# Block mask by matmul for the first two chunks, a second order of the batch 0 loads, and one PSUM tensor with planned banks

## The chip, the cores and the metric

The kernel runs on one core of a Trainium2 chip. The metric is the device time of one execution in microseconds (us), and the number given for a kernel is the median over its runs. The profile comes from one execution of its own. Its span is counted from the first to the last instruction, so it is a little shorter than the time of the same execution.

Engines are named as in the profile: PE multiplies matrices (PEld are its weight loads), DVE is the vector engine, ACT the scalar engine with the activation functions, POOL is GpSimd, SP issues transfers.

## What is computed

Block-sparse attention is followed by a gated feed-forward network (FFN). There are 4 batches, 8 heads, 768 tokens and a head dimension of 64. Tokens form 24 blocks of 32, and a mask says which block may see which: neighbours, the first and the last block, and three sampled blocks for each row of blocks, known only at run time.

```
scores = q @ k.T / 8
mask   = |blk_i - blk_j| <= 1  or  blk_i, blk_j in {0, 23}  or  blk_j sampled for blk_i
attn   = softmax(where(mask, scores, -1e9))
x      = (attn @ v), heads side by side             # 3072 x 512
out    = (sigmoid(x @ w_gate) * (x @ w_val)) @ w_out # 512 -> 1536 -> 512
```

## The kernel before, in words

**Tiles.** Queries are handled in 12 chunks of 256 (`n`), three for each batch (`c`). A chunk has four pairs of heads (`p`), and for each pair three tiles of keys (`tt`). One score group is `attend`'s `scores` (L545): four matmuls with 64 contraction rows, two heads in the two halves of the array, into a tile `st` of two PSUM banks. ACT takes the exponential of the whole group (L555) into `pt`. DVE multiplies `pt` by `mask`, which holds 0 or 1 for each key and query of the chunk's place in its batch (L563). After three groups PE multiplies by V (`values`, L577, 24 matmuls), where a column of ones gives the sum for the softmax. DVE divides (L585, L588). The result is turned to `xT` by PE in the first three chunks (L613, copied by ACT or DVE at L618 or L624), and by a transposing transfer on SP in the others (L601).

**FFN.** It runs chunk by chunk (`ffn`): 12 pairs of gate and value products (L651), a tanh on ACT (L670), a product on DVE (L677), then output matmuls (L695), a scaled copy to `y` (L708, L712) and a store (L717).

**The mask.** DVE compares the sampled block numbers (`blocks`, L461 to L469) into a 24 x 24 block mask `mb16`. Two matmuls (L477) widen its columns to queries, casts (L484) bring that to SBUF as `mb24`, and `spread` (L490) widens the rows to keys, with the 0/1 table `e24` as weights. Copies at L509 (first chunk) and L523 (the other two) bring it to `mask`.

**Batch 0.** K and Q come pair by pair on POOL's queue, cast to f16 on the way (`load_half`, L379), in the order K, Q, K, Q and so on. V comes on SP's queue in f32, each load after the K load of its pair has landed (`load`, L340), and POOL casts it (L355). PE transposes K and Q (`turn_pe`, L391) and DVE or ACT copies them out (L395, L396). The FFN weights follow on POOL's queue (L432, L441). Later batches are loaded in f32 on SP's queue, after one of the `w_out` loads has landed, then cast (L360, L362, L369, L371) and turned by transposing transfers (L405).

**What sets the order.** Every step is handed to a planner (`Plan`) with an engine, an assumed duration, its reads and writes, a priority and, for a transfer, a cost. The planner (`run`) plays them through in its own model time and then emits the instructions in that order. So the order on every engine's queue is fixed before the chip runs, and an engine that waits for a step holds up all behind it. Lower priority numbers go first. FFN steps have large ones and fill the gaps. While nothing else is ready and model time is below `SPIN` (45), PE gets spin matmuls on a tile of zeros (`spin_op`, L325), which compute nothing. A step in mode `row` (the scores) that follows one in mode `full` has to find both `st` tiles free (L173 to L180), so that two groups go together.

**PSUM.** Two `st` tiles of two banks, used in turn, and four single tiles `bank`, of which the planner takes the one that is free first.

Of the kernel before, what the change touches and what calls it, by code (L numbers as in the profile page):

```python
# [16 lines left out]
BLK = 32  # L17
# [8 lines left out]
SCALE = 1.0 / 8.0  # L26
VW = 66
SPIN = 45.0
# [5 lines left out]
class Buf:  # L34


    def __init__(self, ring, make):
        self.ring, self.make = ring, make
        self.users, self.writers = [], []
        self.tile = self.turn = self.slot = None  # L40

# [6 lines left out]
class Op:  # L48
    def __init__(self, ways, deps, allocs, prio, mode, dma, behind):
        self.ways, self.deps, self.allocs = ways, deps, allocs  # L50
        self.prio, self.mode, self.dma, self.behind = prio, mode, dma, list(behind)
        self.eng = self.start = self.end = self.seen = None

# [4 lines left out]
class Plan:  # L58
# [8 lines left out]
    def ring(self, name, n, in_order=True):  # L67


        self.rings[name] = [None] * n  # L70
        if in_order:
            self.queued[name] = 0
# [21 lines left out]
    def run(self):  # L94
# [8 lines left out]
        at = {r: 0 for r in self.rings}  # L103
# [13 lines left out]
        def places(allocs, eng):  # L117

            t, where, taken = 0.0, [], set()
            for b in allocs:  # L120
                if b.ring in self.queued:
                    s = slot(b.ring, 0, eng) if b.turn == at[b.ring] else None
                    where.append(at[b.ring] % len(self.rings[b.ring]))
                else:
                    ring = self.rings[b.ring]
                    can = [
                        (s, ring[i] is self.spun, i)
                        for i in range(len(ring))
                        if i not in taken and (s := clear(ring[i], eng)) is not None
                    ]  # L130
                    can = [(max(s, now), sp, i) for s, sp, i in can]
                    s, _, i = min(can) if can else (None, 0, None)
                    taken.add(i)
                    where.append(i)
                if s is None:
                    return None, None
                t = max(t, s)
            return t, where

        def take(o, where):  # L140
            for b, i in zip(o.allocs, where):
                self.rings[b.ring][i] = b
                b.slot = i
                at[b.ring] += 1
# [3 lines left out]
        while left:  # L148
            wake = []
            for e in LAT:  # L150
# [4 lines left out]
                for o in todo[e]:  # L155
# [17 lines left out]
                    if o.mode == "row" and mode == "full":  # L173
                        s = slot("st", 1)
# [8 lines left out]
                if best is None and e == "PE" and now < self.spin_until and self.spin.writers[0].seen is not None:  # L183
                    if self.spin.writers[0].seen <= now:
                        fresh = self.spun is None or self.rings["bank"][self.spun.slot] is not self.spun
# [51 lines left out]
def kernel(  # L237
# [15 lines left out]
    e24_np = (tok.reshape(1, -1) // BLK == np.arange(NB)[:, None]).astype(np.float16)  # L253
# [18 lines left out]
    for name, n in (  # L272
        ("qs", 3), ("ks", 3), ("vs", 3), ("q16", 4), ("k16", 4), ("qT", 8), ("kT", 8),
        ("v16", 8), ("pt", 12), ("rz", 2), ("x16", 4), ("tg", 2), ("y", 3),
        ("st", 2), ("bank", 4),
    ):
        P.ring(name, n, name != "bank")
# [9 lines left out]
    def psb(tag, shape, dt=f32):  # L287
        if tag == "bank":
            return Buf(tag, lambda i: ps.tile(shape, dt, tag=f"bank{i}", bufs=1, name=f"bank{i}"))
        n = len(P.rings[tag])  # L290
        return Buf(tag, lambda i: ps.tile(shape, dt, tag=tag, bufs=n, name=tag))

    def one(shape, dt, name):
# [8 lines left out]
    e24 = one([NB, NJ, 128], f16, "e24")  # L302
# [5 lines left out]
        "ACT", 0.4, lambda: nc.scalar.dma_start(e24().rearrange("b j q -> b (j q)"), e24_h.ap()),  # L308
        writes=[e24], prio=-88, dma=0.1,
    )  # L310
    P.op("ACT", 0.4, lambda: nc.scalar.dma_start(ident16(), id_h.ap()), writes=[ident16], prio=-87, dma=0.2)
# [8 lines left out]
    def spin_op(dur, fresh):  # L320
        if fresh:
            P.spun = psb("bank", [128, 128])
# [27 lines left out]
    def cast_v(b, p, prio):  # L350
        s, t = stage["v", b, p], vring[(b * NP + p) % 8]
        v16[b, p] = t
        if b == 0:
            P.op(
                "POOL", 0.85, lambda: nc.gpsimd.tensor_copy(t()[:, :, :, 0:64], s()),  # L355
# [18 lines left out]
    def load_half(nm, b, p, prio):  # L374
        c = sb(f"{nm}16", [128, 2, NJ, 64], f16)
        half16[nm, b, p] = c

        def go():
            landed[nm, b, p] = nc.gpsimd.dma_start(c(), src[nm][b][:, 2 * p : 2 * p + 2])  # L379

        return P.op("POOL", 0.75, go, writes=[c], prio=prio, dma=1.02)

    def turn_pe(nm, b, p, prio):
        c, t = half16[nm, b, p], sb(f"{nm}T", [128, NJ, 128], f16)
        tr[nm, b, p] = t
        g = psb("bank", [128, NJ, 128], f16)

        def go():
            for j in range(NJ):
                for hd in range(2):  # L390
                    nc.tensor.transpose(g()[hd * 64 : hd * 64 + 64, j, :], c()[:, hd, j], ident16())  # L391

        P.op("PE", 0.36, go, reads=[c, ident16], writes=[g], prio=prio, mode="col")
        P.op(
            "DVE", 0.55, lambda: nc.vector.tensor_copy(t(), g()), reads=[g], writes=[t], prio=prio,  # L395
            alt=[("ACT", 0.8, lambda: nc.scalar.copy(t(), g()))] if p == 0 else (),  # L396
# [11 lines left out]

    for p in range(NP):
        for i, nm in enumerate("kq"):  # L410
            o = last_in = load_half(nm, 0, p, -60 + 2 * p + i)
            if nm == "k":
                load("v", 0, p, -50 + p, after=[o], sync=("k", 0, p))
    for p in range(NP):
        for i, nm in enumerate("kq"):
            turn_pe(nm, 0, p, -40 + 2 * p + i)
        cast_v(0, p, -40 + 2 * p)
# [39 lines left out]
    mb16 = one([NB, NB], f16, "mb16")  # L457
    mb24 = [one([NB, n, 128], f16, f"mb24_{n}") for n in (2, 4)]
    mask = one([128, NCH, NCH, 512], f16, "mask")

    def blocks():  # L461
# [7 lines left out]
        d.tensor_tensor(mb16(), eqs()[:, 0], eqs()[:, 1], op=ALU.max)  # L469

    P.op("DVE", 0.65, blocks, reads=[sbi, mi], writes=[mb16, eqs], prio=-70)
    mask_ops = {}
    for c, j0, n, eng, dur in ((0, 0, 2, "ACT", 0.37), (1, 2, 4, "DVE", 0.6)):
        p24 = psb("bank", [NB, n, 128])
        P.op(
            "PE", 0.1 * n,
            lambda p24=p24, j0=j0, n=n: nc.tensor.matmul(  # L477
                p24(), mb16(), e24()[:, j0 : j0 + n], start=True, stop=True
            ),
            reads=[mb16, e24], writes=[p24], prio=-69 + c, mode="full",  # L480
        )
        f = nc.scalar.copy if eng == "ACT" else nc.vector.tensor_copy
        P.op(
            eng, dur, lambda p24=p24, j0=j0, n=n, f=f, c=c: f(mb24[c]()[:, 0:n], p24()),  # L484
            reads=[p24], writes=[mb24[c]], prio=-69,
        )

    def spread(c, tt, pm):
        for jj in range(2):
            nc.tensor.matmul(  # L490
                pm[:, jj * CH : (jj + 1) * CH], e24()[:, 2 * tt + jj],
                mb24[0]()[:, 0:2] if c == 0 else mb24[1]()[:, 2 * c - 2 : 2 * c],
                start=True, stop=True,
            )

    first = psb("st", [128, 2, 512]), psb("bank", [128, 512])

    def spread_first():
        for tt in range(2):
            spread(0, tt, first[0]()[:, tt])  # L500
        spread(0, 2, first[1]())

    P.op("PE", 1.2, spread_first, reads=[e24, mb24[0]], writes=first, prio=-69.5, mode="full")
    for tt in range(NCH):
        eng, t = ("DVE", first[0]) if tt < 2 else ("ACT", first[1])
        f = nc.scalar.copy if eng == "ACT" else nc.vector.tensor_copy
        mask_ops[0, tt] = P.op(
            eng, 0.62,
            lambda t=t, tt=tt, f=f: f(mask()[:, 0, tt], t()[:, tt] if tt < 2 else t()),  # L509
            reads=[t], prio=-68 if tt == 0 else -39.5,  # L510
        )

    def build_mask(c, prio, after=()):
        for tt in range(NCH):
            pm = psb("bank", [128, 512])

            P.op(
                "PE", 0.25, lambda tt=tt, pm=pm: spread(c, tt, pm()), reads=[e24, mb24[1]], writes=[pm],
                after=after, prio=prio, mode="full",
            )  # L520
            mask_ops[c, tt] = P.op(
                "DVE", 0.62,
                lambda tt=tt, pm=pm: nc.vector.tensor_copy(mask()[:, c, tt], pm()),  # L523
                reads=[pm], prio=prio - 20,
            )

# [6 lines left out]

    def attend(n, p, seq):
        b, c = divmod(n, NCH)
        pts = []
        for tt in range(NCH):
            st, pt = psb("st", [128, 2, 512]), sb("pt", [128, 2, 2, CH], f16)

            def scores(tt=tt, st=st):  # L540
                qT, kT = tr["q", b, p](), tr["k", b, p]()
                for jj in range(2):
                    for hd in range(2):
                        r = slice(hd * 64, hd * 64 + 64)
                        nc.tensor.matmul(  # L545
                            st()[:, hd, jj * CH : (jj + 1) * CH],
                            kT[r, 2 * tt + jj, :],
                            qT[r, 2 * c : 2 * c + 2, :],
                            start=True, stop=True,
                        )  # L550

            P.op("PE", 0.215, scores, reads=[tr["q", b, p], tr["k", b, p]], writes=[st], prio=seq, mode="row")
# [14 lines left out]
            P.op("DVE", 0.61, masks, reads=[pt], writes=[pt], after=[mask_ops[c, tt]], prio=seq)  # L567
            pts.append(pt)

        o, rz, x16 = psb("bank", [128, 4, VW]), sb("rz", [128, 4, 1], f32), sb("x16", [128, 2, 128], f16)  # L570

# [200 lines left out]
```

## Time and profile before

| | us |
|---|---|
| median of 13 runs | 305.11 |
| lowest, highest run | 304.43, 308.09 |
| the profiled execution, its time | 304.43 |
| its span | 302.6 |
| first score matmul starts | 11.5 |
| first gate matmul starts | 37.8 |
| from here on PE has FFN matmuls only | 252 |
| PE, ACT, DVE busy in the span | 295.4, 209.9, 201.9 |

The profile lists groups of instructions as: line, engine, operation, what is written from what is read, shapes, count, then busy time, mean duration in ns, and the idle time ahead of them with what ended it. The row of 40 slices gives the busy share of each engine in tenths, a slice being 7.6 us. PEclk is the clock that PE was granted, in tenths of full speed. Matmuls are pipelined: the duration of one in the profile is longer than the distance to the next, so rates are read from start to start.

### The profile page before, as it was taken

What the parts mean: (1) busy time and instruction counts of PE and PEld (TensorE: products, weight loads), DVE (VectorE), ACT (ScalarE), POOL (GpSimd) and SP (SyncE); (2) the same over time, 40 slices, a digit from 0 to 9 for tenths busy, and PEclk for the clock granted to TensorE, in tenths of its full rate; (3) what the DMA queues carried; (4) which work ended last, traced back from release to release, by engine and by line L of the source; (5) the groups of instructions that cost most, each with busy time, mean ns of one, the idle gap of its engine ahead of it and who ended that gap; (6) DMA issues with size and microseconds to landing.
All of it is one profiled execution on the core that took longest, in us unless ns stands there. A gap on an engine that the chain in (4) does not pass through costs nothing.

```text
span 302.6 us, 8261 instructions
## 1 busy us (share of the span) xinstructions
PE 295.4 (98%) x3472; PEld 214.5 (71%) x3472; DVE 201.9 (67%) x450; ACT 209.9 (69%) x328; POOL 17.9 (6%) x27
## 2 busy tenths in 40 slices
PE   7898999999999999999999999999999999999995
PEld 6565788587578578668667758757857868778673
DVE  2589888798788777577677767758666664424230
ACT  3388799588978879787777768767877883334331
POOL 8563000000000000000000000000000000000000
PEclk9599999999999999999999999999999999999999
DMA  7999999999999923650020020021011012030001
GB/s 94 243 236 206 207 264 297 230 338 315 280 326 244 221 80 75 150 145 11 17 89 3 19 85 6 6 66 37 2 44 63 2 22 84 12 96 2 35 37 69
DMA packets 52321, 36.00 MB, mean 119 GB/s; under 512 B 31140, under 2 KB 49340, under 8 KB 52284
## 3 DMA queue, kind: packets, MB, share of 16 engines
q1 hardware_dynamic: 44048, 29.11, 35.6%
q0 software_dynamic: 7984, 6.29, 13.5%
q8 instruction: 27, 0.44, 0.6%
q10 hardware_dynamic: 252, 0.08, 0.3%
q14 instruction: 10, 0.08, 0.1%
HBM read 28.39 MB, written 6.29 MB: 115 GB/s over the span
## 4 chain that ended last, share of the span: by engine, by line
PE 92%; DVE 3%; DMA 2%; POOL 1%; issue 0%; ACT 0%; POOLq 0%
PE bank L651 41%; PE bank L695 21%; PE st L545 13%; PE bank L577 12%; DMA k<-in_k_dram 2%; DVE pt L563 2%; PE st L651 2%; PE bank L325 2%; PE bank L391 1%; DVE mask L523 1%; PE bank L613 1%; POOL k L379 1%; POOL q L379 0%; DVE x L588 0%; PE bank L490 0%
## 5 line engine op out<-in xcount | busy, mean ns | idle before, releaser
L555 ACT ACTIVATE pt<-st 128x1024 f16<-128x1024 f32 x144 | 143.3, 1025 | 41.7 <-PE st L545 41.5
L563 DVE TENSOR_TENSOR pt<-pt,mask 128x1024 f16<-128x1024 f16 x144 | 100.2, 702 | 40.8 <-ACT pt L555 40.2
L651 PE MATMUL bank<-x,wv 128*128 128x256 f16 x552 | 83.1, 273 | 0.0
L651 PE MATMUL bank<-x,wg 128*128 128x256 f16 x552 | 82.9, 273 | 0.0
L677 DVE SCALAR_TENSOR_TENSOR h<-tg,bank 128x256 f16<-128x256 f32 x138 | 55.1, 416 | 24.7 <-ACT tg L670 24.6
L695 PE MATMUL bank<-wo,h 128*128 128x512 f16 (+1 forms) x300 | 68.1, 371 | 0.0
L670 ACT ACTIVATE tg<-bank 128x256 f32<-128x256 f32 x138 | 52.0, 389 | 19.5 <-PE bank L651 19.1
L651 PEld LDWEIGHTS <-wv 128*128 128x128 f16 x576 | 54.1, 98 | 11.6 <-issue 5.5
L651 PEld LDWEIGHTS <-wg 128*128 128x128 f16 x576 | 53.8, 98 | 10.2 <-issue 3.4
L695 PEld LDWEIGHTS <-h 128*128 128x128 f16 x300 | 27.5, 98 | 28.3 <-issue 3.3
L545 PE MATMUL st<-qT,kT 64*128 64x256 f16 x576 | 46.7, 275 | 0.0
L577 PEld LDWEIGHTS <-pt 128*128 128x128 f16 x1152 | 42.0, 98 | 4.8 <-issue 1.9
L577 PE MATMUL bank<-v,pt 128*128 128x65 f16 x1152 | 44.4, 193 | 0.0
L545 PEld LDWEIGHTS <-kT 64*128 64x128 f16 x576 | 21.3, 94 | 18.0 <-issue 14.3
L588 DVE TENSOR_TENSOR x<-bank,rz 128x256 f16<-128x256 f32 x48 | 20.4, 424 | 4.0 <-DMA x<-x 2.5
L712 ACT ACTIVATE y<-bank 128x512 f32<-128x512 f32 (+1 forms) x13 | 7.3, 565 | 17.6 <-PE bank L695 17.5
L325 PE MATMUL bank<-zero 128*128 128x128 f16 x152 | 14.4, 251 | 1.0 <-DVE zero L304 1.0
L585 DVE RECIPROCAL rz<-bank 128x4 f32<-128x4 f32 x48 | 8.5, 178 | 9.1 <-PE bank L577 9.1
L325 PEld LDWEIGHTS <-zero 128*128 128x128 f16 x152 | 11.0, 113 | 4.7 <-issue 3.8
L708 DVE TENSOR_SCALAR y<-bank 128x512 f32<-128x512 f32 x12 | 8.2, 685 | 1.7 <-PE bank L695 1.7
L362 ACT CAST v<-vs 128x768 f16<-128x768 f32 x7 | 5.9, 837 | 0.4 <-PE bank L577 0.4
L371 ACT CAST k<-ks 128x768 f16<-128x768 f32 x6 | 5.1, 848 | 0.0
(46 smaller groups left out, 81.0 us busy)
## 6 DMA issues: line engine op xcount, KB each, us to landing
vs<-in_v_dram SPq DMA_DIRECT2D x16, 384.0 KB, 6.0
out_dram<-y SPq DMA_DIRECT2D x23, 256.0 KB, 2.2
ks<-in_k_dram SPq DMA_DIRECT2D x12, 384.0 KB, 5.0
qs<-in_q_dram SPq DMA_DIRECT2D x12, 384.0 KB, 4.8
wo<-in_moe_w_out_dram POOLq DMA_DIRECT2D x3, 512.0 KB, 17.6
wg<-in_moe_w_gate_dram POOLq DMA_DIRECT2D x2, 512.0 KB, 14.0
wv<-in_moe_w_val_dram POOLq DMA_DIRECT2D x2, 512.0 KB, 15.6
k<-in_k_dram POOLq DMA_DIRECT2D x4, 192.0 KB, 6.1
```

Source lines behind the costliest of these rows:

```text
L325: "PE", dur, lambda: nc.tensor.matmul(t(), zero(), zero(), start=True, stop=True),
L545: nc.tensor.matmul(st()[:, hd, jj * CH : (jj + 1) * CH], kT[r, 2 * tt + jj, :], qT[r, 2 * c : 2 * c + 2, :], start=True, stop=True,)
L555: lambda st=st, pt=pt: nc.scalar.activation(pt().rearrange("p h j q -> p h (j q)"), st(), AF.Exp, scale=SCALE),
L563: nc.vector.tensor_tensor(t, t, mask()[:, c, tt].unsqueeze(1).to_broadcast([128, 2, 512]), op=ALU.mult)
L577: nc.tensor.matmul(o()[:, 2 * jq + hd, 0:65], pts[j // 2]()[:, hd, j % 2, jq * 128 : jq * 128 + 128], v_[:, hd, j, 0:65], start=(j == 0), ...
L585: P.op("DVE", 0.2, lambda: nc.vector.reciprocal(rz(), o()[:, :, 64:65]), reads=[o], writes=[rz], prio=seq - 5)
L588: lambda: nc.vector.tensor_tensor(x16().rearrange("p j (h d) -> p (j h) d", d=64), o()[:, :, 0:64], rz().to_broadcast([128, 4, 64]), op=AL ...
L651: nc.tensor.matmul(t()[:, z : z + w], wt()[:, i, f * 128 : (f + 1) * 128], xT[g, i]()[:, 0:w], start=(i == 0), stop=(i == NP - 1),)
L670: lambda tg=tg, a=pair[0]: nc.scalar.activation(tg()[:, 0:w], a[0]()[:, a[1] : a[1] + w], AF.Tanh, scale=0.5),
L677: lambda tg=tg, a=pair[1], h_=h_: nc.vector.scalar_tensor_tensor(h_()[:, 0:w], tg()[:, 0:w], 1.0, a[0]()[:, a[1] : a[1] + w], op0=ALU.add, ...
L695: nc.tensor.matmul(py()[:, m], hts[g, f]()[:, tt * 128 : (tt + 1) * 128], wo()[:, f, m], start=(f == 0), stop=(f == NF - 1),)
L708: lambda py=py, y=y, m=m: nc.vector.tensor_scalar_mul(y()[:, m], py()[:, m], 0.5),
```

## The change

- In the chunks 0 and 1 (`NMASK`) the mask is no longer multiplied. A matmul with `e24` as weights and a new tile `bias` (0 where a block may be seen, -16384 where not) writes `st` first, and the score matmul accumulates on it. `e24` and `bias` are laid out twice, in the rows 0 to 23 and 64 to 87, one for each half of the array. The multiplication stays for the chunks from 2 on; `mask` is now made from the bias, by matmuls of the same count, for the second place of a batch, the third, and last the first.
- Score groups of the first two chunks go without waiting for two free tiles; those of chunk 0 have a third pair of banks.
- Batch 0's Q is loaded in two pieces for all heads: the part for chunk 0 second of all loads, the rest last. V is loaded on POOL's queue with a cast to f16, between the K loads, and DVE copies it into place. `e24` (now 128 rows) and the identity move from ACT's queue to SP's.
- PSUM is one tensor; the planner gives each tile its bank from a list of homes: the banks 0 to 3 as two pairs for scores, 4 to 7 single; the last groups of the FFN may use all eight.
- Copies of turned `x` and of turned K and Q are on DVE alone. `SPIN` is 22. The value step of chunk n is put behind the last gate step of chunk n-2.

The diff, cut to its core (the planner's bookkeeping of banks is left out):

```
-SPIN = 45.0
+BIG = 16384.0
+SPIN = 22.0
+NMASK = 2
...
-                    if o.mode == "row" and mode == "full":
-                        s = slot("st", 1)
+                    if o.mode == "row" and mode == "full" and o.paired:
+                        s, _ = places([o.allocs[0], o.twin], e)
...
-    e24_np = (tok.reshape(1, -1) // BLK == np.arange(NB)[:, None]).astype(np.float16)
+    e24_np = np.zeros((128, NJ * 128), np.float16)
+    for r in (0, 64):
+        e24_np[r : r + NB] = tok.reshape(1, -1) // BLK == np.arange(NB)[:, None]
...
+    psum = ps.tile([128, 8, 512], f32, name="psum")
+    SINGLE, PAIR = (7, 6, 5, 4), (0, 2)
...
+        "SP", 0.5, lambda: nc.sync.dma_start(e24().rearrange("b j q -> b (j q)"), e24_h.ap()),
+        writes=[e24], prio=-92, dma=0.5,
...
+    P.op("SP", 0.5, lambda: nc.sync.dma_start(ident16(), id_h.ap()), writes=[ident16], prio=-91, dma=0.3)
...
-                "POOL", 0.85, lambda: nc.gpsimd.tensor_copy(t()[:, :, :, 0:64], s()),
+                "DVE", 0.3, lambda: nc.vector.tensor_copy(t()[:, :, :, 0:64], s()),
...
+    qc0, qc12 = one([128, H, 2, 64], f16, "qc0"), one([128, H, 4, 64], f16, "qc12")
     for p in range(NP):
-        for i, nm in enumerate("kq"):
-            o = last_in = load_half(nm, 0, p, -60 + 2 * p + i)
-            if nm == "k":
-                load("v", 0, p, -50 + p, after=[o], sync=("k", 0, p))
+        hs = slice(2 * p, 2 * p + 2)
+        tr["q", 0, p], tr["k", 0, p] = sb("qT", [128, NJ, 128], f16), sb("kT", [128, NJ, 128], f16)
+        c = sb("k16", [128, 2, NJ, 64], f16)
+        load_half(c, "k", hs, slice(0, NJ), -60 + 2 * p, 1.02)
+        if p == 0:
+            load_half(qc0, "q", slice(0, H), slice(0, 2), -59.5, 1.5)
+        turn_pe(c, 0, tr["k", 0, p], slice(0, NJ), -40 + p)
+        turn_pe(qc0, 2 * p, tr["q", 0, p], slice(0, 2), -39.5 + p)
     for p in range(NP):
-        for i, nm in enumerate("kq"):
-            turn_pe(nm, 0, p, -40 + 2 * p + i)
-        cast_v(0, p, -40 + 2 * p)
+        stage["v", 0, p] = t = sb("q16", [128, 2, NJ, 64], f16)
+        load_half(t, "v", slice(2 * p, 2 * p + 2), slice(0, NJ), -57.5 + 2 * p, 1.02)
+        cast_v(0, p, -38.5 + p)
+    last_in = load_half(qc12, "q", slice(0, H), slice(2, NJ), -50, 2.6)
...
+    for c, j0, n in ((0, 0, 2), (1, 2, 4)):
+        pb = psb([n, 128])
         P.op(
             "PE", 0.1 * n,
+            lambda pb=pb, j0=j0, n=n: nc.tensor.matmul(
+                pb(), mb16(), e24()[0:NB, j0 : j0 + n], start=True, stop=True
             ),
+            reads=[mb16, e24], writes=[pb], prio=-69 + 31 * c, mode="full",
+        )
         P.op(
+            "DVE", 0.1 + 0.13 * n,
+            lambda pb=pb, j0=j0, n=n: nc.vector.tensor_scalar(
+                bias()[:, j0 : j0 + n], pb(), -1.0, BIG, op0=ALU.add, op1=ALU.mult
+            ),
+            reads=[pb], writes=[bias], prio=-69 + 31 * c,
+        )
...
+    def build_mask(c, prio):
+        for tt in range(NCH):
+            pm = psb([512])
+            def spread(tt=tt, pm=pm):
+                for jj in range(2):
+                    nc.tensor.matmul(
+                        pm()[:, jj * CH : (jj + 1) * CH], e24()[0:64, 2 * tt + jj],
+                        bias()[0:64, 2 * c : 2 * c + 2], start=True, stop=True,
+                    )
+            P.op("PE", 0.22, spread, reads=[e24, bias], writes=[pm], prio=prio, mode="row")
+            mask_ops[c, tt] = P.op(
+                "DVE", 0.65,
+                lambda tt=tt, pm=pm: nc.vector.tensor_scalar(
+                    mask()[:, c, tt], pm(), 1.0 / BIG, 1.0, op0=ALU.mult, op1=ALU.add
+                ),
+                reads=[pm], prio=prio,
             )
...
+        masked = n < NMASK
...
+            st, pt = psb([2, 512], homes=(0, 2, 4) if n < 1 else PAIR, span=2), sb("pt", [128, 2, 2, CH], f16)
...
+                    for own in (0, 1) if masked else (1,):
+                        for hd in range(2):
+                            r = slice(hd * 64, hd * 64 + 64)
+                            l, m = (kT, qT) if own else (e24(), bias())
+                            nc.tensor.matmul(
+                                st()[:, hd, jj * CH : (jj + 1) * CH],
+                                l[r, 2 * tt + jj, :],
+                                m[r, 2 * c : 2 * c + 2, :],
+                                start=not (own and masked), stop=bool(own),
+                            )
...
+            o.paired, o.twin = not masked, psb([2, 512], homes=PAIR, span=2)
...
-            P.op("DVE", 0.61, masks, reads=[pt], writes=[pt], after=[mask_ops[c, tt]], prio=seq)
+            if not masked:
+                P.op("DVE", 0.61, masks, reads=[pt], writes=[pt], after=[mask_ops[c, tt]], prio=seq)
...
+        if n == 1:
+            for p in range(NP):
+                turn_pe(
+                    qc12, 2 * p, tr["q", 0, p], slice(2, NJ), 2.0
+                )
+            for c_, pr in ((1, 11.5), (2, 13.5), (0, 26)):
+                build_mask(c_, pr)
...
+    for (n, p), o in valued.items():
+        g = group_of[n][0] - 2
+        if g >= 0:
+            o.behind.append(gates[2 * NF * (g + 1) - 1])
```

## The prediction

> **What bounds the kernel now.** I read the page's shares first, then its row of 40 slices.
>
> ```profile
> PE 295.4 (98%) x3472; PEld 214.5 (71%) x3472; DVE 201.9 (67%) x450; ACT 209.9 (69%) x328; POOL 17.9 (6%) x27
> ...
> PE   7898999999999999999999999999999999999995
> ...
> DVE  2589888798788777577677767758666664424230
> ...
> PEclk9599999999999999999999999999999999999999
> ```
>
> PE looks full all the time, and only the second slice ran at half clock. But part of that filling is dummy work: the spin matmuls of L325. So I cut the span where the gate matmuls begin (37.8), and asked for each engine, and then for L325 alone.
>
> ```profile
> 0.00:11.50 11.50, 8.81 (x107) 7.08 (x107) 4.55 (x19) 3.03 (x4) 8.99 (x16) 0.89 0.89 136
> 11.50:37.80 26.30, 25.24 (x406) 17.25 (x405) 22.29 (x42) 20.08 (x23) 8.95 (x11) 0.92 1.26 224
> 37.80:252.00 214.20, 214.20 (x2592) 153.91 (x2591) 159.41 (x353) 168.60 (x258) 0.00 (x0) 1.00 0.47 122
> 252.00:299.20 47.20, 47.19 (x373) 36.30 (x371) 15.60 (x37) 17.79 (x43) 0.00 (x0) 1.00 0.13 46
> ```
>
> ```profile
> 0.00:11.50 11.50, 4.34 (x39) 0.89 0.89 136
> 11.50:37.80 26.30, 10.09 (x113) 0.92 1.26 224
> 37.80:252.00 214.20, 0.00 (x0) 1.00 0.47 122
> ```
>
> The columns of the first are PE, PEld, DVE, ACT, POOL; of the second PE alone. In 11.5 to 37.8 there are 113 spins, while DVE is busy 22.3 of 26.3 us. From 37.8 there are none. The timeline of PE gives the rate of each kind of matmul and the price of going to the scores and back.
>
> ```profile
> 142.37 0.60 PE L651 MATMUL bank<-x,wg 128*128 128x256 f16 x4
> 142.90 0.61 PE L545 MATMUL st<-qT,kT 64*128 64x256 f16 x8
> 143.44 0.61 PE L651 MATMUL bank<-x,wv 128*128 128x256 f16 x4
> 143.89 0.92 PE L577 MATMUL bank<-v,pt 128*128 128x65 f16 x24
> 144.66 0.60 PE L651 MATMUL bank<-x,wg 128*128 128x256 f16 x4
> ```
>
> From start to start, four gate matmuls take 0.437 (0.109 each), 24 value matmuls 0.77, and a score group of four (two run side by side) 0.218. Eight scores should take 0.44, but 0.53 passes before them where 0.44 is due and 0.54 behind: about 0.2 for a visit to the scores. The other rates, read likewise: output matmuls of 512 columns 0.216, transposes of q and k 0.044, of x 0.055.
>
> The ledger of PE. From 37.8 to the last matmul's end (299.2) it has 1152 gates (125.8), 276 outputs of 512 and 24 of 256 columns (62.2), 122 score groups (26.6), 42 value groups (32.6) and 14 turns (0.8): 248.0 of 261.4. The rest, 13.4, is 61 visits at 0.22. So nothing waits after 37.8: PE is the bound there, with no slack to win. Up to 37.8 useful work is 98 transposes (4.3), the mask matmuls (2.3), 22 score groups (4.8), 6 value groups (4.65) and 10 turns (0.55), 16.6; so 21.2 us are lost, 8 of them before the first score at 11.5. This is all that the change can win, and every matmul that it adds is paid in full in the end.
>
> Who holds the middle up:
>
> ```profile
> L555 ACT ACTIVATE pt<-st 128x1024 f16<-128x1024 f32 x144 | 143.3, 1025 | 41.7 <-PE st L545 41.5
> L563 DVE TENSOR_TENSOR pt<-pt,mask 128x1024 f16<-128x1024 f16 x144 | 100.2, 702 | 40.8 <-ACT pt L555 40.2
> ...
> L545 PE MATMUL st<-qT,kT 64*128 64x256 f16 x576 | 46.7, 275 | 0.0
> ```
>
> In 11.5 to 37.8 ACT waits 8.6 us for scores and DVE 1.8 for exps. DVE has the mask multiplications (14.3 of its 22.3), six mask casts (L523), the value tail and copies; chunk 0's x is complete only at 36.
>
> **Part by part.**
>
> *Bias matmuls.* They replace 24 DVE multiplications of 0.70 (0.755 in this stretch), 16.8 to 18 us of DVE. They add 96 matmuls in 24 groups of four, two side by side as in L545: 24 x 0.218 = 5.2 us of PE. At half clock a masked group takes 0.87 and a visit, about an exp. Where PE idles today the 5.2 hide in spin time; since PE is full later, I charge them in full and count the idle time that goes separately.
>
> *Visits.* The rule that waits for two free score buffers is off for masked groups, so most of the 24 are visits of their own. TensorEngine Tiling (Performance and key properties, under Tiling Modes) says that a change of tiling mode drains TensorE. It gives no figure; the row above does, 0.2. Bias and score share a mode, so no switch lies between them. Had each bias needed its own switch, 24 x 0.2 = 4.8 more would come and the change would lose; I take none.
>
> *Loads.* K of pair 0 landed at 5.96 (issued 1.23), then pieces of 192 KB followed 1.1 to 1.45 apart. Now all heads' Q of chunk 0 comes second: 256 KB in 1024 rows of 512 bytes, halved by the cast. By bytes it takes 1.5 to 1.9 us. DMA: Bandwidth & Descriptors (Specifications) asks for 512 bytes at least for full rate, which speaks against this piece. If a short row cost what one of queue 0 costs today (13.5% of 16 engines' 302.6 us over 7984 packets, 82 ns), it would be 1024 x 82 / 16 = 5.2 us. Queue 1's packets, mostly short ones, take 39 ns: 2.5 us. I take 2.5: the page counts 31140 of 52321 packets under 512 bytes, and queue 0 has only 7984 in all, so queue 1's row is the one that is made of short packets. With 0.2 for the larger block table on SP ahead of it, Q lands at 8.7, and after transposes and copy the first score runs at 9.6 (8.7 by bytes, 12.3 by the slow price). That is 1.9 earlier, but only about 1.3 of useful work precedes it (3.4 today), so 8.3 are lost there against 8.1: no gain by itself.
>
> *V on the cast queue.* The same bytes are read from DRAM. SP's four V loads and POOL's four casts (0.84 to 1.35) go; POOL held its later weight issues at 13.3 behind such a cast. DVE gets four casts: 0.3 to 0.56 each, 1.2 to 2.2 us, in room that the multiplications leave. POOL issues ten loads at 0.72 instead of eight ahead of the weights, 1.4 us; it was waiting for landings anyway. Weights follow the same volume, so the first landing stays near 20 (the first output load waits for it until 19.2) and the later gate pieces at 30 to 34 (issued 14.6 to 17.0, 16 to 17 to landing): from -1 to +2 us, taken as 0.
>
> *Masks.* Nine casts instead, of 0.68 as today, with three for chunk 0 needed only in batch 1; two bias evacuations replace two casts. These 18 matmuls equal today's. x copies all on DVE: seven of 0.38 leave ACT, seven of 0.29 come. All fit DVE's room; without it, 2 us.
>
> *PSUM and order.* The steady state keeps two score pairs and four single banks; its 60 visits stay. Holding the values of chunk n behind the gates of n-2 reorders PE work that has no slack: 0, between -1 and +1. Shorter spins (plan time 22 for 45) cost nothing if gates fill PE by then.
>
> *What is late next: ACT, then PE.* Exps start at 10.3 and take 12 x 1.025 = 12.3; about 1.5 of gaps while the clock is at half brings 24. Values, reciprocal, product, turn and copy (3 us as in the timeline today) give x at 27 instead of 36, and gates start, weights being there from 20. In 9.6 to 27 PE does 12 masked groups (5.2), 4 value groups (3.1), 80 transposes (3.5), turns (0.4) and three groups of chunk 1 (1.3), 13.5 of 17.4: 3.9 lost to half clock, visits and waits. Then nine single visits (1.8, of which today pays 0.2), and 0.5 for gates whose weights land at 30 to 34. Sum of the losses: 8.3 + 3.9 + 1.6 + 0.5 = 14.3. Today's 21.2 minus the added 5.2 is 16.0. Gain 1.7 us: span 302.6 to 300.9, profiled execution 304.4 to 302.7, and from the median of 305.1 to 303.4. The median lies 0.7 above the profiled one, and I let the gain be the same.
>
> **Rivals.**
>
> *The idle time only becomes bias work (0.23).* If chunk 0's x comes at 28.5, or the waits in between are 1.5 more, the gain is 0 to 0.9: 304.8. For it: PE's demand in 9.6 to 27 is 13.5 plus up to 2.4 of visits plus 2 to 3 of half clock, hardly less than the room.
>
> *The second Q load blocks PE's order (0.22).* The remaining Q (512 KB) comes tenth, behind V. Its 32 transposes stand in PE's fixed order among chunk 0's scores, at the place where the planner believes it landed (its costs give 15.4: 2.1 + 1.1 for small loads + 8 x 1.02 + 1.5 + 2.6); the real landing, ten pieces at 1.2 plus short rows, is 19 to 22. Everything behind on PE waits, the scores of pair 3 first, and so ACT. From about 20 each us is one us of loss; at 23, 3.5 us: 305.1 - 1.7 + 3.5 = 306.9, slower. Against it: exps run slower than the planner's 0.915, so PE arrives late there, at about 19.
>
> *PE stays warm and full (0.15).* The clock today is 0.50 from 9.0 to 15.6. TensorE: Matmul & The Clock Gate (Part 1) has the clock halved by an idle window of 3.4 us and given back by a busy one. If the first window passes, or ends at 12.4, 1.5 to 2 us return, and with Q by bytes 0.8 more: gain 4.3, 300.8.
>
> The likeliest case, a gain of about 1 to 3 us, has 0.40.
>
> **How the numbers follow.** About 0.3%, 0.9 us, is what a measurement can tell here: faster means below 304.2. Likeliest case and warm PE are faster: 0.55, with a little of the second rival's mild end 0.57. The first rival is the same, 0.22. Slower 0.21. The range reaches from the warm case, with 0.5 beyond, to the blocked order: 300.3 to 307.0. The likeliest one's own range is 302.0 to 304.2.
>
> **What would show it.** Right: no L563 among the first 24 exps; first exp near 10.3; ACT almost gapless to 24; the first L651 near 27 and PE without waits from there; 672 matmuls at the scores' line; score visits of four in the first two chunks. Wrong: a wait of PE for the second Q load above 1 us; first score after 11; gates starting after 30; a clock below 1 after 16; or a gap between bias and score matmuls of the size of a switch. A gain above 5 us would mean that my ledger of PE misses something in the full stretch after 37.8.

## The result and the profile after

| | before | after |
|---|---|---|
| median, us | 305.41 (48 runs, 304.17 to 308.87) | 302.58 (11 runs, 301.45 to 307.11) |
| ratio after / before | | 0.9895, interval 0.9863 to 0.9926 |
| the profiled execution, its span | 304.43, 302.6 | 303.60, 301.8 |
| first matmul of a score group, first exp | 11.53, 12.18 | 10.58, 11.66 |
| first gate matmul | 37.8 | 30.9 |

The changed kernel is faster: 2.8 us by the medians, 3.2 by the ratio (1.05% of 305.4), where 1.7 was predicted. The ratio leaves out the two longest runs of after (306.68 and 307.11), which fell in a slower state of the chip. The profiled pair is only 0.8 apart: the profiled run of after lies 1.0 above its median, that of before 1.0 below its own. So the traces show less gain than the medians.

The page of after, shares and rows of 40 slices:

```profile
PE 292.4 (97%) x3455; PEld 214.8 (71%) x3455; DVE 185.0 (61%) x434; ACT 213.1 (71%) x330; POOL 16.1 (5%) x25
...
PE   6899999999999899999999999999999999999995
...
DVE  3477357889687477756757847747747747634330
...
PEclk9599999999999999999999999999999999999999
```

DVE has 17 us less. PE's row now has an 8 in the fourteenth slice (98 to 106), where before had a 9. Its groups of instructions show what replaced what:

```profile
L575 ACT ACTIVATE pt<-psum 128x1024 f16<-128x1024 f32 x144 | 144.1, 1024 | 41.3 <-PE psum L560 41.2
L583 DVE TENSOR_TENSOR pt<-pt,mask 128x1024 f16<-128x1024 f16 x120 | 82.7, 691 | 53.0 <-ACT pt L575 52.6
...
L560 PE MATMUL psum<-qT,kT 64*128 64x256 f16 x576 | 51.0, 275 | 1.7 <-ACT pt L575 1.7
...
L560 PE MATMUL psum<-bias,e 64*128 64x256 f16 x96 | 14.0, 292 | 0.0
```

24 multiplications are gone, 96 bias matmuls have come, and the scores wait 1.7 us for exps, where before had 0.0. The busy time by stage, cut at the first score and the first gate of this kernel (columns PE, PEld, DVE, ACT, POOL), then the spins alone (PE and PEld):

```profile
0.00:10.50 10.50, 6.93 (x81) 5.78 (x81) 3.41 (x22) 1.28 (x1) 8.46 (x15) 0.88 0.98 131
10.50:30.90 20.40, 20.20 (x350) 15.20 (x346) 14.02 (x35) 15.85 (x17) 7.60 (x11) 0.90 1.34 202
30.90:252.00 221.10, 218.68 (x2591) 158.63 (x2590) 148.60 (x333) 175.75 (x270) 0.00 (x0) 1.00 0.51 126
```

```profile
0.00:10.50 10.50, 4.34 (x39) 3.87 (x39) 0.88 0.98 131
10.50:30.90 20.40, 0.00 (x0) 0.00 (x0) 0.90 1.34 202
```

The 113 spins of the stretch before the gates are gone. DVE is busy 14.0 of 20.4 us there, where it was busy 22.3 of 26.3. But between 30.9 and 252 PE is idle for 2.4 us, where before was idle for none after its first gate. 0.6 of them lie ahead of 60, the other 1.8 in one place, here in the timeline of PE:

```profile
98.20 0.93 PE L598 MATMUL psum<-v,pt 128*128 128x65 f16 x24
99.06 0.61 PE L560 MATMUL psum<-qT,kT 64*128 64x256 f16 x8
99.61 2.76 PE L704 MATMUL psum<-wo,h 128*128 128x512 f16 x12
103.15 0.40 PE L560 MATMUL psum<-qT,kT 64*128 64x256 f16 x4 [0.78 <-ACT pt L575]
104.07 0.39 PE L560 MATMUL psum<-qT,kT 64*128 64x256 f16 x4 [0.52 <-ACT pt L575]
104.39 1.04 PE L704 MATMUL psum<-wo,h 128*128 128x512 f16 x4
105.27 0.92 PE L598 MATMUL psum<-v,pt 128*128 128x65 f16 x24
106.03 1.02 PE L704 MATMUL psum<-wo,h 128*128 128x512 f16 x4
106.99 0.39 PE L560 MATMUL psum<-qT,kT 64*128 64x256 f16 x4
107.81 0.39 PE L560 MATMUL psum<-qT,kT 64*128 64x256 f16 x4 [0.43 <-ACT pt L575]
108.31 0.60 PE L660 MATMUL psum<-x,wg 128*128 128x256 f16 x4
```

From 96.5 to 108.3 there is not one gate matmul (L660). The gates of chunks 0 to 2, 288 in all, are done, and those of chunk 3, the first of batch 1, have not begun. Before has the same gap from 99.5 to 108.0, filled to the last by outputs, values and scores, without a wait:

```profile
105.82 0.61 PE L545 MATMUL st<-qT,kT 64*128 64x256 f16 x8
106.36 1.04 PE L695 MATMUL bank<-wo,h 128*128 128x512 f16 x4
107.24 0.93 PE L577 MATMUL bank<-v,pt 128*128 128x65 f16 x24
108.00 0.60 PE L651 MATMUL bank<-x,wg 128*128 128x256 f16 x4
```

So the changed kernel is 3.0 us ahead at the gap's start and not ahead at all at its end. PE's three waits there, 1.7 us in all, are for exps. On ACT's queue these stand behind casts of batch 3's K and Q, which wait for their loads:

```profile
99.01 0.83 ACT L393 CAST k<-ks 128x768 f16<-128x768 f32 x1 [0.77 <-DMA ks<-in_k_dram]
101.35 0.83 ACT L393 CAST q<-qs 128x768 f16<-128x768 f32 x1 [1.51 <-DMA qs<-in_q_dram]
102.08 1.93 ACT L575 ACTIVATE pt<-psum 128x1024 f16<-128x1024 f32 x2
```

DVE's queue holds the first gate matmul of chunk 3 in the same way. The profile names the division at L609 as what released it at 108.31 (L609 reads a PSUM tile, which is then free), and that division stood behind the cast of batch 3's last K, which landed at 107.05:

```profile
107.15 0.56 DVE L391 CAST k<-ks 128x768 f16<-128x768 f32 x1 [2.12 <-DMA ks<-in_k_dram]
...
107.83 0.42 DVE L609 TENSOR_TENSOR x<-psum,rz 128x256 f16<-128x256 f32 x1
```

The gates of chunk 3 need its x too, and that is to be read on SP's queue:

```profile
93.16 1.17 SPq L622 DMA_TRANSPOSE x<-x  x1
94.77 0.39 SPq L362 DMA_DIRECT2D vs<-in_v_dram  x1
95.22 0.45 SPq L362 DMA_DIRECT2D ks<-in_k_dram  x1
95.73 0.46 SPq L362 DMA_DIRECT2D qs<-in_q_dram  x1
...
98.33 0.83 SPq L362 DMA_DIRECT2D ks<-in_k_dram  x1
99.25 0.90 SPq L362 DMA_DIRECT2D qs<-in_q_dram  x1
100.25 4.49 SPq L622 DMA_TRANSPOSE x<-x  x3
```

From chunk 3 on, x is turned by a DMA of SP, not by PE. DVE writes the last x of chunk 3 from 90.3; SP turns it at 100.25, behind nine loads of 384 KB in a row. They are batch 3's, whose scores begin at 193.2. The trace of that one transpose says when it landed:

```profile
L622 SPq DMA_TRANSPOSE x<-x x1: 1895/1895/1895, 100.3 to 100.3; - x1
...
DMA to landing us min/median/max: 8.2/8.2/8.2
```

It landed at 108.45, and the fourth gate matmul of chunk 3, which needs it, starts at 108.63. It follows the third without a wait, so in this execution PE waited for exps and for DVE, and x alone would have let it start only about 0.1 us sooner. The casts and x alike came late with the same nine loads. The transpose issued at 93.16, ahead of the loads, had taken 2.3. In before the same x is written from 92.28 and issued at 98.48: 6.2 later instead of 10.0.

### The profile page after: what moved, and what is told of

Its sections match the earlier page's. It is cut to its first block, busy times and chain, and to the rows that moved or that the text cites. A ratio compares the mean times of both kernels' runs of the same rounds, so it can differ in the third digit from the quotient of the medians.

```text
span 301.8 us, 8196 instructions
## 1 busy us (share of the span) xinstructions
PE 292.4 (97%) x3455; PEld 214.8 (71%) x3455; DVE 185.0 (61%) x434; ACT 213.1 (71%) x330; POOL 16.1 (5%) x25
## 4 chain that ended last, share of the span: by engine, by line
PE 77%; DMA 17%; DVE 1%; SPq 1%; POOL 1%; issue 1%; ACT 0%; DVEq 0%; POOLq 0%
PE psum L660 39%; PE psum L704 19%; PE psum L560 10%; PE psum L598 9%; DMA ks<-in_k_dram 6%; DMA wo<-in_moe_w_out_dram 6%; DMA wv<-in_moe_w_val_dram 3%; DMA qc<-in_q_dram 2%; SPq L362 1%; DVE k L391 0%; DVE pt L583 0%; ACT pt L575 0%; DVE x L609 0%; POOL qc L398 0%; POOL k L398 0%
## 5 line engine op out<-in xcount | busy, mean ns | idle before, releaser
L575 ACT ACTIVATE pt<-psum 128x1024 f16<-128x1024 f32 x144 | 144.1, 1024 | 41.3 <-PE psum L560 41.2
L583 DVE TENSOR_TENSOR pt<-pt,mask 128x1024 f16<-128x1024 f16 x120 | 82.7, 691 | 53.0 <-ACT pt L575 52.6
L660 PE MATMUL psum<-x,wv 128*128 128x256 f16 x576 | 86.8, 273 | 0.0
L660 PE MATMUL psum<-x,wg 128*128 128x256 f16 x576 | 86.6, 273 | 0.1
L686 DVE SCALAR_TENSOR_TENSOR h<-tg,psum 128x256 f16<-128x256 f32 x144 | 56.8, 416 | 21.7 <-ACT tg L679 21.5
L704 PE MATMUL psum<-wo,h 128*128 128x512 f16 (+1 forms) x300 | 67.3, 371 | 0.5 <-DVE h L686 0.5
L679 ACT ACTIVATE tg<-psum 128x256 f32<-128x256 f32 x144 | 55.1, 389 | 13.1 <-PE psum L660 10.2
L660 PEld LDWEIGHTS <-wg 128*128 128x128 f16 x576 | 55.0, 98 | 10.4 <-issue 3.2
L660 PEld LDWEIGHTS <-wv 128*128 128x128 f16 x576 | 53.6, 98 | 12.2 <-issue 6.5
L560 PE MATMUL psum<-qT,kT 64*128 64x256 f16 x576 | 51.0, 275 | 1.7 <-ACT pt L575 1.7
L598 PE MATMUL psum<-v,pt 128*128 128x65 f16 x1152 | 42.5, 193 | 0.2 <-ACT pt L575 0.2
L609 DVE TENSOR_TENSOR x<-psum,rz 128x256 f16<-128x256 f32 x48 | 20.4, 424 | 1.6
```

Source lines behind the costliest of these rows:

```text
L560: nc.tensor.matmul(st()[:, hd, jj * CH : (jj + 1) * CH], l[r, 2 * tt + jj, :], m[r, 2 * c : 2 * c + 2, :], start=not (own and masked), sto ...
L575: lambda st=st, pt=pt: nc.scalar.activation(pt().rearrange("p h j q -> p h (j q)"), st(), AF.Exp, scale=SCALE),
L583: nc.vector.tensor_tensor(t, t, mask()[:, c, tt].unsqueeze(1).to_broadcast([128, 2, 512]), op=ALU.mult)
L598: nc.tensor.matmul(o()[:, 2 * jq + hd, 0:65], pts[j // 2]()[:, hd, j % 2, jq * 128 : jq * 128 + 128], v_[:, hd, j, 0:65], start=(j == 0), ...
L609: lambda: nc.vector.tensor_tensor(x16().rearrange("p j (h d) -> p (j h) d", d=64), o()[:, :, 0:64], rz().to_broadcast([128, 4, 64]), op=AL ...
L660: nc.tensor.matmul(t()[:, z : z + w], wt()[:, i, f * 128 : (f + 1) * 128], xT[g, i]()[:, 0:w], start=(i == 0), stop=(i == NP - 1),)
```

## Experiments

The theory: DVE's multiplications held PE back until 38, the bias matmuls end this, and their own PE time is the price. Rivals: the loads, PSUM plan and order bring the gain (A); the hold of the values makes the stall at 102 to 108 (B); the clock at half speed in 7.9 to 14.7 makes the difference between runs (C); the Q load in two pieces is what helps (D). The first four ran on one chip beside 62 runs of before (median 304.91).

**bias_off.** The bias undone, loads, PSUM plan and order of steps kept. Without the bias the scores of chunks 0 and 1 also wait again for two free tiles, as in before:

```
-NMASK = 2
+NMASK = 0
     seq = 0
+    build_mask(0, -38)
...
-            for c_, pr in ((1, 11.5), (2, 13.5), (0, 26)):
+            for c_, pr in ((1, 11.5), (2, 13.5)):
```

> The change with the bias matmuls undone in both chunks (the 24 multiplications on DVE are back, the mask of the first place is built ahead of chunk 0); loads, PSUM plan and order as changed. My theory: the gain is idle time of PE that DVE's multiplications caused, less 5.2 us of bias matmuls, so PE saves 5.2 here but waits for DVE again: near the kernel before, ratio to it 0.995 to 1.002, first gate matmul at 35 or later. Rival (the gain is from the loads and the order, the bias only costs): 0.985 or less.

Measured 303.53 (302.62 to 305.27), ratio 0.9961 (0.9942 to 0.9980). DVE is busy 17.8 us in 10.5 to 30.9 (14.0 in after). PE's lost time up to 60, counted as in the prediction, is 22.2 us, as in before (22.3), where after has 15.0. But this kernel's clock stays at half speed far longer, as its row of clocks shows:

```profile
PEclk9555999999999999999999999999999999999999
```

Part of the 22.2 may be the clock's, so this run alone doesn't settle rival A. What it bounds is the rest of the change: without the bias 0.4% of gain is left, where the whole shows 1.05% in the first measurement and 0.64% in the control below.

**no_hold.** The last loop of the change (the `valued` and `behind` lines) removed.

> The changed kernel without the rule that holds the values of chunk n behind the gates of n-2. My theory: PE has no slack after 40, so nothing: ratio to the kernel before 0.989 plus or minus 0.003. Rival A (the rule carries the gain): 0.996 or more. Rival B (the rule makes the PE waits of 102 to 108 us that the changed profile shows, about 2 us): these waits are gone and the ratio is near 0.983.

Measured 303.62 (301.87 to 305.31), ratio 0.9960 (0.9940 to 0.9981). The gap between the gates is still there (96.1 to 106.1), and PE still waits 1.9 us in it, for DVE and for x, so rival B falls. From the fourth gate matmul of chunk 3 to the span's end it takes 195.0 us, after 193.2. That the hold saves this 1.8 is not shown: two more score groups are left to do there (340 score matmuls for 332), and bias_off and q_pairs, which keep the hold, take 195.2 and 195.1. In the times it is 0.2 to 0.6% (0.9960 against 0.9936 of the control and 0.9895), and against the control the intervals overlap.

**warm.** 32 dummy matmuls behind the second matmul that makes the bias:

```
+                [
+                    nc.tensor.matmul(psum[:, 0, 0:128], zero(), zero(), start=True, stop=True)
+                    for _ in range(32 * c)
+                ],
```

> The changed kernel with 32 more dummy matmuls right after the two matmuls that make the bias, where PE waits 1.7 us for the Q load; they compute nothing. Theory: the runs of the changed kernel spread from 301.5 to 304.3 with the granted clock (1.00 to 0.987), which drops because of this wait; so all runs now have a clock of 1.00 and lie at 301.5 to 302.4, ratio about 0.988, and first exp at 11.2 instead of 11.7. Rival (the clock is not set by this wait): spread and clock as before, or slower by the part of the dummies that outlasts the wait.

Measured 302.65 (300.74 to 305.46), ratio 0.9916 (0.9888 to 0.9945). The clock is full until 103.1, then at half until 106.5, and chunk 2's gates end at 94.1, 2.4 us sooner than in after; those of chunk 3 begin at 107.3, only 1.0 sooner. The runs with a mean clock of 0.998 or more still lie from 300.74 to 304.39, so rival C falls as the whole cause of the spread. In this profile most of the time won ahead of the gap is lost in it: PE waits 1.9 us for exps there. That the clock has a part is not excluded: in the first measurement of after five runs with a mean clock of 1.00 took 301.45 to 302.37, and two with 0.987 and 0.988, one of them profiled, 304.26 and 303.60.

**q_pairs.** Q of batch 0 loaded pair by pair in whole rows behind its K, V still on POOL's queue:

```
-        if p == 0:
-            load_half(qc0, "q", slice(0, H), slice(0, 2), -59.5, 1.5)
+        qf = one([128, 2, NJ, 64], f16, f"qf{p}")
+        load_half(qf, "q", hs, slice(0, NJ), -59.5 + 2 * p, 1.02)
...
```

> The changed kernel with batch 0's Q loaded pair by pair in whole rows behind each K, as in the kernel before, V still on the cast queue between them. My theory: the first score comes 1 to 1.5 us earlier (Q of pair 0 lands near 7.1, not 8.4), but K of the later pairs lands later, so exps get gaps before 20; in all within 1 us of the changed kernel, ratio 0.987 to 0.993. Rival (the two-piece Q load carries the gain): 0.996 or more.

Measured 302.93 (301.82 to 303.99), ratio 0.9932 (0.9906 to 0.9957): not to be told from after. The Q load in two pieces is not what helps, and rival D falls.

The next four ran on another chip (before: 305.19, 19 runs).

**after_again.** The changed kernel once more, unedited, as the control of this group.

> The changed kernel itself, as the control of this group and once more for its ratio: 0.9895 as measured, 0.986 to 0.993. It is compared with the other three here, which run on the same chip.

Measured 304.13 (301.37 to 307.04), ratio 0.9936 (0.9900 to 0.9972). Its profile is worth more than its time. It is the same program as after; its profiled execution took 305.36 for 303.60, 1.76 more, and the fourth gate of chunk 3 starts at 110.37 for 108.63, 1.74 later. Behind that gate both take 193.2. The whole difference between two executions of one kernel arises ahead of that one gate. In both traces the releases lead back from that gate's group to batch 3's last K: it landed at 108.80 for 107.05, 1.75 later, and the first gate matmul of chunk 3 follows it by 1.25 and 1.26 us. PE waited 3.0 us for exps in the gap, where after waited 1.7.

**nmask1, nmask3.** Only chunk 0 masked by bias, or the first three chunks: `NMASK = 1`, `NMASK = 3`.

> The changed kernel with the bias in chunk 0 only; chunk 1 is multiplied by DVE again. My theory: PE loses 2.6 us of bias work (12 x 0.218), but DVE gets 12 x 0.70 = 8.4 us in 23 to 40, where it is busy 60% in the changed kernel, so there is room for most of it: within 1.5 us of the changed kernel, on either side. Rival (relief of DVE is what pays, in both chunks alike): half of the way back to bias_off, and its loss against the changed kernel is half of that one's.

> The changed kernel with the bias in chunk 2 as well. My theory: there PE is full, so 12 x 0.218 = 2.6 us are paid whole and the DVE time gained (8.4 us) is worth nothing: slower than the changed kernel by 2 to 3 us, near the kernel before. Rival (DVE relief pays wherever it is): faster than the changed kernel.

nmask1: 301.28 (300.63 to 302.51), ratio 0.9840 (0.9799 to 0.9881), faster than both kernels. Lost PE time up to 60 is 15.0, equal to after's, with 2.7 us more useful work done: the bias of chunk 1 costs its full price and wins nothing. Here PE waits for x itself at the gap's end:

```profile
103.82 0.49 PE L660 MATMUL psum<-x,wg 128*128 128x256 f16 x3 [0.26 <-DVE y L717]
105.11 0.27 PE L660 MATMUL psum<-x,wg 128*128 128x256 f16 x1 [0.80 <-DMA x<-x]
```

Three gate matmuls run on the first three pairs' x, the fourth waits for the DMA that turns the last x.

nmask3: 312.99 (312.34 to 313.54), ratio 1.0218 (1.0176 to 1.0259), far worse than expected. Chunk 2's gates end at 95.4, still 1.0 sooner than in after, so the additional bias matmuls are not the damage. Chunk 3's last x comes from DVE only at 109.1 (90.3 in after), its gates start at 113.1, and PE has lost 26.0 us by 120. SP issues batch 3's loads in another order here (from 80.6 to 98.5, between the transposes), and of chunk 3's 12 exps the ninth (the 45th of all) starts at 73.6 but the tenth, which waits for its scores, only at 101.3. Why the planner arranged it so was not followed up.

**deep_stage.** Four buffers in place of three for each of the staged loads: `("qs", 4), ("ks", 4), ("vs", 4)`.

> The changed kernel with four instead of three f32 staging buffers for each of K, Q, V of the later batches. Theory: the waits at 102 to 108 us of the changed profile (PE 1.7 us and lone score groups) come from nine of these loads that SP issues in one burst at 94.8 to 99.3 behind a transpose, so that DVE and ACT stand at their casts until 107; with one more buffer loads go out earlier, the waits shrink and 1 to 1.6 us are won against the changed kernel. Rival (the waits come from PE's own order there): the waits stay, nothing is won.

Measured 302.07 (299.68 to 302.50), ratio 0.9851 (0.9806 to 0.9895). The scores wait 0.2 us for exps in place of 1.7. It seemed that a deeper ring cures the burst of loads, so the last group (before: 304.44, 40 runs) put it on trial.

**one_deep, one_deep_warm, before_deep.** nmask1 with the four buffers, the same with warm's dummies, and before with four buffers.

> Bias in chunk 0 only, and four staging buffers for each of K, Q, V. Theory: the two gains are of different places (2.6 us of bias matmuls that win nothing in chunk 1; the waits at 102 to 108 us) and add up: nmask1 less 1 to 2 us, ratio to the kernel before 0.977 to 0.981. Rival (both took away the same waits): as nmask1, 0.984.

> one_deep with the 32 dummy matmuls where PE waits for the Q load. Theory: the clock stays at 1.00 until 100, and PE, which runs masked groups in chunk 0, gains 0.5 to 1.5 us against one_deep. Rival (in chunk 0 ACT and the loads set the pace, so a faster PE only waits): within 0.4 us of one_deep.

> The kernel before with four staging buffers for each of K, Q, V and nothing else. It has no waits at 100 to 110 us in its profile, so if the gain of deep_stage is the waits that the change brought, nothing is won here: ratio 0.998 to 1.002. Rival (a further staging buffer helps in general): 0.995 or less.

one_deep: 304.14 (302.08 to 306.17), ratio 0.9976 (0.9952 to 1.0001), where two gains were to add up. one_deep_warm: 303.40, ratio 0.9958 (0.9939 to 0.9977). before_deep: 304.71, ratio 1.0010 (0.9984 to 1.0036). So buffers are not the cure, and the theory of the deeper ring falls. PE of one_deep shows why nmask1's gain is gone:

```profile
106.41 0.50 PE L660 MATMUL psum<-x,wg 128*128 128x256 f16 x3
107.54 0.37 PE L660 MATMUL psum<-x,wg 128*128 128x256 f16 x1 [0.63 <-DMA x<-x]
```

It is the same wait, 2.4 us later than in nmask1, and the spans are 2.8 apart. The last x of chunk 3 was written from 87.6 here and from 87.0 in nmask1, but SP issued its transpose at 101.4 behind six loads, in nmask1 at 97.4 behind seven. The scores ahead of these gates waited 2.2 us for exps, in nmask1 0.4.

**no_bias1.** nmask1 without its 48 bias matmuls: `for own in (1,)`, `start=True, stop=True`. It leaves out the mask of chunk 0 altogether.

> nmask1 with the bias matmuls of chunk 0 left out too, in the same order of work; chunk 0 is then not masked at all. It prices the bias where PE still has idle time. By my ledger (every bias matmul is paid in the end): 2.6 us below nmask1, about 298.7. Rival (in chunk 0 they lie in time that PE idles anyway): as nmask1, within 0.8 us.

Measured 300.49 (299.15 to 302.02), ratio 0.9855 (0.9822 to 0.9889), against 0.9840 of nmask1. Lost PE time up to 60 is 17.8 for 15.0: what the bias leaves, idle time takes. The two ran on different chips, but their profiles agree too: the 288 gates are done at 93.5 and 93.4, ahead of the gap, the fourth gate of chunk 3 starts at 105.1 in both, and the spans are 298.9 and 299.0. So the bias of chunk 0 is free, which was not expected.

**The profiles side by side.** Times in us from the traces: when the last gate of chunks 0 to 2 starts; when DVE begins to write the last x of chunk 3; when SP issues its transpose; when the fourth gate of chunk 3 starts; what remains from there to the span's end.

| | last of 288 gates | last x | transpose | fourth gate | rest | span |
|---|---|---|---|---|---|---|
| before | 99.5 | 92.3 | 98.5 | 108.3 | 194.3 | 302.6 |
| bias_off | 98.2 | 95.1 | 98.7 | 107.1 | 195.2 | 302.3 |
| after | 96.5 | 90.3 | 100.3 | 108.6 | 193.2 | 301.8 |
| after_again | 96.8 | 90.6 | 101.6 | 110.4 | 193.2 | 303.6 |
| no_hold | 96.1 | 89.2 | 99.4 | 107.4 | 195.0 | 302.4 |
| warm | 94.1 | 87.9 | 98.4 | 107.7 | 193.2 | 300.9 |
| q_pairs | 95.6 | 91.3 | 97.6 | 105.1 | 195.1 | 300.2 |
| nmask1 | 93.4 | 87.0 | 97.4 | 105.1 | 193.9 | 299.0 |
| no_bias1 | 93.5 | 87.1 | 98.3 | 105.1 | 193.9 | 298.9 |
| deep_stage | 94.3 | 91.2 | 100.8 | 106.7 | 193.6 | 300.3 |
| one_deep | 94.1 | 87.6 | 101.4 | 107.5 | 194.2 | 301.8 |
| one_deep_warm | 93.3 | 87.1 | 101.3 | 108.3 | 193.7 | 302.0 |
| before_deep | 102.2 | 95.1 | 101.5 | 110.7 | 194.3 | 305.0 |
| nmask3 | 95.4 | 109.1 | 109.6 | 113.7 | 196.9 | 310.6 |

Without nmask3 the rest varies by 2.0 us, the fourth gate by 5.6, and the first column by 8.8. Among the variants the order of the spans is mostly that of the fourth gate, not of the first column: warm and one_deep finish chunk 2's gates as early as nmask1 does and end 1.9 and 2.8 later. But what PE waited for ahead of that gate differs. In no_hold, q_pairs, nmask1, deep_stage, one_deep and one_deep_warm the fourth gate waits 0.3 to 0.8 us for x. In after, after_again, warm, no_bias1 and nmask3 it does not, and PE waited 1.0 to 5.0 us for exps. In before, before_deep and bias_off PE waits for nothing there. Nor is the rest always the same work: 328 to 356 score matmuls are left at the fourth gate. This is one execution of each, read afterwards. What was not tried is the direct test: turning chunk 3's x on PE, its transpose ahead of the loads, or batch 3's loads and casts later.

## Why the prediction was right, and where its steps were not

The direction, the likeliest case and its range (302.0 to 304.2) held; both medians of the changed kernel, 302.58 and 304.13, lie in it. The cause was right, but that the number fits is in part luck: the sum has compensating errors.

- **DVE held the middle up: right.** 21.2 lost us up to the gates were to become 14.3; counted alike at 60, they went from 22.3 to 15.0, that is 7.3 where 6.9 was predicted. The trace agrees stage by stage (DVE 22.3 of 26.3 to 14.0 of 20.4), and nmask1 against bias_off, 0.9840 to 0.9961, says that chunk 0's bias does it, with the reservations that bias_off's clock was at half for longer and that its scores wait for two free tiles again. Rival A is left with the 0.4% of bias_off.
- **First score at 9.6, first exp at 10.3: late by 1.0 and 1.4.** The choice among the prices of the Q piece was right: it landed at 8.4 for 8.7, where the slow price that was weighed would have given 11.4. It took 2.9 us behind K where 2.5 was taken, and K came 0.4 sooner (5.54, in before 5.91). The step that failed is what stands behind it: PE's fixed order has Q's turns and K's second pair ahead, and the latter waits for its load. PE after, in that stretch:

```profile
8.47 0.85 PE L410 MATMUL psum<-ident,qc 128*64 128x128 f16 x12 [1.55 <-DMA qc<-in_q_dram]
9.59 0.85 PE L410 MATMUL psum<-ident,k 128*64 128x128 f16 x12 [0.26 <-DMA k<-in_k_dram]
10.23 0.42 PE L410 MATMUL psum<-ident,qc 128*64 128x128 f16 x4
10.58 0.40 PE L560 MATMUL psum<-bias,e 64*128 64x256 f16 x2
10.77 0.42 PE L560 MATMUL psum<-qT,kT 64*128 64x256 f16 x2
```

- **Gates at 27: they came at 30.9**, beyond the mark of 30 that was set as a sign of failure, and yet the lost time was recovered as forecast. 1.4 of the 3.9 is the later first exp; the rest was not taken apart.
- **Visits and switches: mild.** Bias and score follow at the pace of two scores (10.58 to 10.77 at half clock), so no switch lies between them, as assumed; most groups went by twos, so single visits cost less than the 1.6 counted.
- **"Every matmul that it adds is paid in full in the end": failed for half of them.** Chunk 0's 2.6 us are free (no_bias1), chunk 1's are paid (nmask1). A chunk that another engine or a load holds back has room on PE; chunk 1 runs when gates can fill PE.
- **"So nothing waits after 37.8: PE is the bound there, with no slack to win", and the order at "0, between -1 and +1": the largest miss.** It was true of before, where PE had work of its own up to 108.0. But what PE does from there on hangs on batch 3's loads, through their casts in the queues of ACT and DVE, and on x through DVE, SP and a DMA. Both were due at nearly the same time, and the ledger of PE couldn't see a chain that ends just in time. PE came 3.0 sooner to the gap, the gates of chunk 3 came 0.3 later, and 1.8 us of idle time appeared there. At the gap's end the profiled pair is level by the clock. What is left of the gain, 1.1 us, is behind the gap: 194.3 became 193.2. Most of this is work done sooner: 332 score matmuls are left there for 340, two groups and two visits, which by the ledger's rates is about 0.9 (an estimate).
- **Rivals.** The second Q load did not block: its turns ran at 20.64 without a wait. PE did not stay warm in the profiled execution: half clock lasted from 7.9 to 14.7. In five of the runs it did, with a mean clock of 1.00. That the bias merely takes the place of idle time and wins nothing is what chunk 1 shows.

Why the median gain of the first measurement lies above the predicted 1.7 stays open. The executions shorter than the profiled one may have kept a full clock or passed the gap sooner; no trace shows one of them.

## What to carry to other kernels

Here work put on the bounding engine was free in a stage where another engine bounds and was paid in full in the next, so a change like this is weighed chunk by chunk: with the rest of the change one chunk was worth 1.6%, two about 0.6 to 1.1%, and three cost 2.2%, in the trace through the order of steps and not through the bias matmuls. An engine that shows no wait may still have a chain that ends just as it needs it; before a gain is carried forward, list the next places where its work needs something from elsewhere (the first tile of the next batch), and how much later than needed each would be. Look at where prefetches stand in the queues: here a small transfer on the path landed 8.2 us after its issue behind nine of them and 2.3 ahead of them, and casts of data that is not needed for 90 us more held exps and a PSUM tile until their loads landed.

## What the runs showed of the hardware

- A DMA that turns one x (128 x 256) landed after 2.3 us ahead of the nine loads of 384 KB and after 8.2 us behind them (8.6 in after_again, 7.7 behind seven loads in nmask1), issued on the same queue. Waiting behind them and sharing bandwidth with them were not told apart.
- Two executions of one program differed by 1.76 us, and all but 0.02 arose ahead of one gate matmul, with the same 193.2 us behind it.
- Keeping the clock full from the start (warm) brought chunk 2's gates forward by 2.4 us and left the median where it was (302.65 for 302.58).
